# One tile per double chunk for the gated unit's input, and an order of its own for the first four double chunks

## The chip, the cores and the metric

The kernel runs on one core of a Trainium2 chip. A core has engines that run on their own and wait for one another by semaphores: TensorE (PE: matmuls and transposes, with its weight loads shown apart as PEld), VectorE (DVE), ScalarE (ACT), GpSimd (POOL) and SyncE (SP), which here only issues transfers. Matmuls write to PSUM[...]; everything else lies in SBUF. The metric is the device time of one execution in microseconds, a median of several. The span of a profiled execution, from its first to its last instruction, is a little shorter than its time.

## The reference

Eight batches, eight heads, 576 tokens, head size 64. Attention without softmax: scores are weighted by a decay per head and cut causally. Its output is laid out as x with 512 features, and a gated unit follows. The gate is a causal convolution over five tokens, so it needs the four tokens ahead of each stretch.

```python
scores = scale * (q @ k.transpose(0, 1, 3, 2))             # q, k, v: (8, 8, 576, 64)
gamma = 1 - 2.0 ** (-5.0 - arange(8))                      # one decay per head
ret = scores * where(rel >= 0, gamma ** rel, 0)            # rel = query position - key position
x = (ret @ v).transpose(0, 2, 1, 3).reshape(8, 576, 512)

xp = concatenate([zeros((8, 4, 512)), x], axis=1)
gate = sigmoid(sum(conv_w[k] * xp[:, k:k + 576] for k in range(5)))
out = (gate * (x @ w_val)) @ w_out                         # float32
```

## The kernel before

Work is cut into 18 double chunks, numbered m. A batch has two full ones of 256 tokens, and the four batches of a group share one of tails (4 x 64 tokens), so m = 8 and m = 17 are tails and the others are full. For a full one, each half `ab` of 128 tokens has masked scores within the half, and a running state of all halves before it for the rest.

For each m:

- `load` and `cast_*`: q, k, v arrive as float32 and become bfloat16, mostly on POOL; v is multiplied by a decay (`gin`).
- `turn`, `take_turned`: TensorE transposes k and q into PSUM and ACT copies them out (`kq`).
- `scores`, `masks`: 16 small matmuls into two banks, and DVE multiplies by the mask.
- `update`, `take_state`: the state grows by k times v of a half; ACT copies it out (`sd`, `sl`).
- `carried`, `values`: state times q, and masked scores times v, into the banks `o`.
- `take_x`: DVE multiplies `o` by the decay of the query (`gout`) and writes x as bfloat16.

One iteration later `conv` (the convolution, as matmuls with diagonal matrices `dg`), `gate`, `value` (x times w_val, then times the gate) and `project` (times w_out) follow. So iteration m mixes the attention of m with the gated unit of m-1 and the projection of m-2. The program's order on each engine is the order written here.

In the code `dcs[m]` gives (kind, batch or group, c), and c is the position of a full chunk in its batch: 0 at even and 1 at odd m in the first group; in the second group, after the tail, 0 at odd and 1 at even m.

```python
P, HP, W, PAD, GB, R = 128, 64, 256, 4, 4, 2      # W: tokens of a double chunk; PAD: leading tokens; GB: batches of a group
NP, NCH, TAIL, LB = 4, 2, 64, 4                   # NP: pairs of heads; NCH: full double chunks of a batch; LB: buffers of a load
# PSUM pools: ps_t, ps_s, ps_o, ps_st have one bank for each tile name; ps_g has two banks
    xg = [xp.tile([P, GB, NP, PAD + S], BF16, name=f"xg{g}") for g in range(B // GB)]
# ... (cut)
    def prep_wv(copy, part):
        src = wvf.rearrange("p o (pr ab hl j) -> p o pr ab hl j", pr=2, ab=2, hl=2)
        for (j0, blk, ab, hl) in ORDER[2 * part:2 * part + 2]:
            copy(wvb[:, :, blk:blk + 2, j0:j0 + HP], src[:, :, :, ab, hl, :])
# ... (cut)
    def take_x(m, ab):
        kind, b, c = dcs[m]
        if kind == "full":
            t0 = c * W + ab * P
            nc.vector.tensor_tensor(
                xg[b // GB][:, b % GB, :, PAD + t0:PAD + t0 + P].rearrange("p o (n r) -> p o r n", r=R),
                ops[m, ab], gout[:, :, t0:t0 + P].rearrange("p o (r n) -> p o r n", r=R), op=ALU.mult)
        else:
            nc.vector.tensor_tensor(
                xg[b][:, ab::2, :, PAD + c * W:PAD + S].rearrange("p b o n -> p o b n"),
                ops[m, ab], gout[:, :, c * W:S].unsqueeze(2).to_broadcast([P, NP, R, TAIL]), op=ALU.mult)
# ... (cut)
    def take_state(m, ab):

        if m >= ND or dcs[m][0] != "full":
            return
        kind, b, c = dcs[m]
        last = ab == 1 and c == NCH - 1
        t = tp_sb.tile([P, NP, D], BF16, name="sl" if last else "sd", bufs=GB if last else 4)
        nc.scalar.copy(t, st[b])
        before[("tail", b) if last else (m, 1) if ab == 0 else (m + 1, 0)] = t

    def xs(n, rows, blk, shift):
        kind, b, c = dcs[n]
        c0 = c * W + shift
        if kind == "full":
            return xg[b // GB][rows, b % GB, blk, c0:c0 + W]
        return xg[b][rows, :, blk, c0:c0 + TAIL]

    gps, gsb, zsb = {}, {}, {}

    def conv(n):

        g = [ps_g.tile([P, 2, 2 * P], F32, name="g") for _ in range(2)][::-1]
        gps[n] = g
        gsb[n] = {}
        lists = [], []
        for pr in range(2):
            a, b = 2 * pr, 2 * pr + 1
            for kk in range(KC):
                for bank, rows, blks in ((0, half[1], (b, a)), (1, half[0], (a, b))):
                    lists[bank].append([mm(g[bank][half[i], pr, :], lhsT=dg[rows, blks[i], kk, :],
                                           rhs=xs(n, rows, blks[i], kk), start=(pr == 0 and kk == 0),
                                           stop=(pr == 1 and kk == KC - 1)) for i in range(2)])
        return lists

    def gate(n, i):
        t = gp.tile([P, 2, 2 * P], F32, name=f"gate{i}")
        nc.scalar.activation(t, gps[n][i], AF.Sigmoid)
        gsb[n][i] = t

    def value(n, i, bank=None):
        vps = (spare(ps_g, "g") if bank is None else bank).rearrange("p (j n) -> p j n", j=2)
        for j in range(2):
            for o in range(NP):
                nc.tensor.matmul(vps[:, j, :], lhsT=wvb[:, o, 2 * i + j, :], rhs=xs(n, slice(0, P), o, PAD),
                                 start=(j == 0 and o == 0), stop=(j == 1 and o == NP - 1), skip_group_check=True)
        z = gp.tile([P, 2, 2 * P], BF16, name=f"z{i}", bufs=3)
        nc.vector.tensor_tensor(z, gsb[n][i], vps, op=ALU.mult)
        zsb[n, i] = z
# ... (cut)
    def keep_warm(n):

        t = ps_t.tile([P, DM], F32, name="tps")
        for _ in range(n):
            nc.tensor.matmul(t, zeros[:, 0:P], zeros, start=True, stop=True)

    keep_warm(8)
    cast_k(0, (v_copy, 4))
    bank = turn(0, 0)
    take_turned(0, 0, bank, (v_copy, 4))
    cast_q(0, (s_copy, 2), (g_copy, 2))
    prep_conv_weights()
    keep_warm(4)
    bank = turn(1, 0, spare(ps_g, "g", [P, NP, R, P], BF16))
    take_turned(1, 0, bank, (s_copy, 2), (v_copy, 2))
    prep_gout(0)
    cast_v(0)
    for o in range(2):
        prep_diagonals(o, nc.vector)
    for (name, f) in (("k", cast_k), ("q", cast_q), ("v", cast_v)):
        f(1)
    for m in range(LB, LB + 2):
        for name in "kqv":
            load(name, m)

    pairs = lambda a: [sum(a[k:k + 2], []) for k in range(0, len(a), 2)]
    for m in range(ND + 1):
        now, unit, nxt, last = ok(m), ok(m - 1), ok(m + 1), m == ND
        soon = m < 2

        if now:
            run(scores(m, 0))
            masks(m, 0, 0)
            masks(m, 0, 1)
        if m == 0:
            keep_warm(4)
            run(update(0, 0))
            take_state(0, 0)
            for o in range(2, NP):
                prep_diagonals(o, nc.vector)
        hi, lo = conv(m - 1) if unit else ([], [])
        if now:
            run(carried(m, 1))
            run(pairs(update(m, 1)), lo[0:2])
            take_state(m, 1)
        else:
            run(lo[0:2])
        run(lo[2:10], hi[0:8])
        if unit:
            gate(m - 1, 1)
        if soon:
            run(hi[8:10])
        else:
            run(pairs(update(m + 1, 0)), hi[8:10])
            take_state(m + 1, 0)
        if unit:
            gate(m - 1, 0)
        if now:
            run(scores(m, 1))
            masks(m, 1, 0)
            masks(m, 1, 1)

        if last:
            value(m - 1, 1, spare(ps_s, "s1"))
            value(m - 1, 0, spare(ps_s, "s0"))
            project(m - 2, 0)
            project(m - 2, 1)
            project(m - 1, 0, last=True)
            project(m - 1, 1, last=True)
            continue
        if m == 1:
            prep_wv(v_copy, 1)
            prep_wv(s_copy, 0)
            value(0, 1)
        if nxt:
            bank = turn(0, m + 1)
            take_turned(0, m + 1, bank)
        if m > 1:
            value(m - 1, 1)
            project(m - 2, 0)
        if ok(m + 2):
            for (name, f) in (("k", cast_k), ("q", cast_q), ("v", cast_v)):
                f(m + 2)
                if ok(m + 2 + LB):
                    load(name, m + 2 + LB)

        run(*values(m, 1))
        run(*values(m, 0))
        run(carried(m, 0))
        take_x(m, 0)
        take_x(m, 1)

        if nxt:
            bank = turn(1, m + 1)
            take_turned(1, m + 1, bank)
        if m == 0:
            prep_gout(1)
            nc.scalar.activation(warm, lsc, AF.Sigmoid)
            load_wo()
        if unit:
            value(m - 1, 0)
        if ok(m - 2):
            project(m - 2, 1)
        if soon:
            run(update(m + 1, 0))
            take_state(m + 1, 0)
```

## Time and profile before

| | before |
|---|---|
| time, median of 3 | 181.7 us (179.49 to 183.25) |
| span of the profiled execution (its time: 180.84) | 179.1 us |
| mean granted TensorE clock | 0.958 of full speed |
| bytes moved, mean rate | 39.81 MB, 222 GB/s |
| of it read, written | 30.42 MB, 9.44 MB |

The costliest groups on the engines, as the page's fifth part gives them (busy time of all, and one instruction's mean):

| operation | engine | count | busy us | one, ns |
|---|---|---|---|---|
| mask times scores (L294) | DVE | 64 | 41.2 | 685 |
| value matmuls (L408, in bank g) | PE | 272 | 37.4 | 277 |
| transposed k, q out of PSUM (L272) | ACT | 34 | 34.6 | 1019 |
| projection (L418) | PE | 111 | 34.7 | 379 |
| v times decay, to bfloat16 (L242) | POOL | 18 | 34.5 | 1916 |
| convolution matmuls (L254, dg) | PE | 720 | 31.4 | 280 |
| decay times o, written as x (L343) | DVE | 32 | 22.3 | 745 |

How to read such a profile: a busy time is the sum of an engine's instructions, and says nothing of when they ran. The rows of 40 slices show when, in tenths of each slice. A row of a timeline has a start, a length, the engine, the line of the program, the operation, what it writes and reads, and how many instructions were merged; in square brackets stands how long the engine was idle before it and whose work it then waited for. TensorE's small matmuls overlap one another, so their single durations don't add up.

### The profile page before, as it was taken

The numbers are of one execution on the slowest core, as the hardware profiler recorded it, in microseconds if no ns is written. First come the engines' busy times: TensorE is split into PE (matmuls) and PEld (weight loads), VectorE is DVE, ScalarE is ACT, GpSimd is POOL, SyncE is SP. The second block draws the span as 40 slices with busy tenths as digits, with TensorE's granted clock in tenths as the row PEclk, the third lists the DMA queues.
The fourth block names the chain that finished last, engine by engine and source line by source line (L and its number), as shares of the span: only waits on it lengthen the run. The fifth ranks groups of instructions, "written<-read, shape, count | busy, mean of one in ns | idle before, by whom it ended". The sixth has DMA issues, their size and how long they took to land.

```text
span 179.1 us, 7593 instructions
## 1 busy us (share of the span) xinstructions
PE 148.3 (83%) x3344; PEld 108.8 (61%) x3377; DVE 105.9 (59%) x191; ACT 93.4 (52%) x154; POOL 74.0 (41%) x69
## 2 busy tenths in 40 slices
PE   7776370889889998998978997999899899989980
PEld 2344270776657685766756775777577576757630
DVE  6468409356566675666445775766667576665320
ACT  3163843256465674665356563756476565633330
POOL 4372499487645446281708263562805000000000
PEclk9999558699999999999999999999999999999998
DMA  4999999999897799999999697876842111111334
GB/s 140 347 321 249 343 287 248 314 299 298 252 254 176 224 330 346 286 344 305 332 345 300 222 289 203 261 227 152 200 168 109 61 65 59 62 62 65 114 117 117
DMA packets 69054, 39.81 MB, mean 222 GB/s; under 512 B 14218, under 2 KB 63902, under 8 KB 69022
## 3 DMA queue, kind: packets, MB, share of 16 engines
q1 hardware_dynamic: 68256, 38.54, 73.2%
q0 software_dynamic: 576, 0.52, 1.8%
q8 instruction: 26, 0.43, 1.0%
q10 hardware_dynamic: 190, 0.27, 0.6%
q14 instruction: 6, 0.05, 0.1%
HBM read 30.42 MB, written 9.44 MB: 222 GB/s over the span
## 4 chain that ended last, share of the span: by engine, by line
PE 74%; DVE 13%; ACT 4%; issue 4%; DMA 2%; ACTq 0%; DVEq 0%
PE g L408 18%; PE g L418 16%; PE g L254 13%; PE tps L264 9%; PE o L308 8%; DVE xg L343 6%; PE s L254 6%; PE st L254 3%; DMA fk<-in_k_dram 2%; DVE wvb L217 2%; DVE p L294 2%; DVE dg L211 2%; ACT gout L187 1%; PE s L408 1%; PE tps L442 1%
## 5 line engine op out<-in xcount | busy, mean ns | idle before, releaser
L294 DVE TENSOR_TENSOR p<-s,mask 128x512 bf16<-128x512 f32 x64 | 41.2, 685 | 22.3 <-PE s L254 22.3
L272 ACT COPY kq<-tps 128x1024 bf16<-128x1024 bf16 x34 | 34.6, 1019 | 23.0 <-PE tps L264 22.8
L408 PE MATMUL g<-xg,wvb 128*128 128x256 bf16 x272 | 37.4, 277 | 10.2 <-DVE xg L343 5.4
L226 POOL CAST qb<-fq 128x1024 bf16<-128x1024 f32 (+1 forms) x18 | 18.3, 1019 | 49.9 <-issue 21.7
L418 PE MATMUL g<-wob,z 128*128 128x512 bf16 x111 | 34.7, 379 | 2.1 <-issue 0.4
L426 ACT COPY ob<-g 128x512 f32<-128x512 f32 x34 | 19.9, 585 | 31.3 <-PE g L418 27.9
L242 POOL TENSOR_TENSOR vb<-fv,gin 128x1024 bf16<-128x1024 f32 x18 | 34.5, 1916 | 3.6 <-DMA fv<-in_v_dram 3.5
L408 PEld LDWEIGHTS <-wvb 128*128 128x128 bf16 x288 | 26.8, 99 | 14.9 <-issue 7.2
L411 DVE TENSOR_TENSOR z<-gate,g 128x512 bf16<-128x512 f32 x34 | 23.4, 687 | 17.6 <-PE g L408 17.6
L254 PE MATMUL g<-xg,dg 64*64 64x256 bf16 x720 | 31.4, 280 | 0.8 <-issue 0.6
L343 DVE TENSOR_TENSOR xg<-o,gout 128x512 bf16<-128x512 f32 x32 | 22.3, 745 | 12.0 <-PE o L308 12.0
L401 ACT ACTIVATE gate<-g 128x512 f32<-128x512 f32 x36 | 21.2, 604 | 13.6 <-DVE p L294 7.1
L254 PEld LDWEIGHTS <-dg 64*64 64x64 bf16 x720 | 24.1, 109 | 3.6 <-issue 3.1
L226 POOL CAST kb<-fk 128x1024 bf16<-128x1024 f32 x17 | 17.8, 1050 | 8.8 <-DMA fk<-in_k_dram 6.7
L418 PEld LDWEIGHTS <-z 128*128 128x128 bf16 x144 | 14.0, 98 | 10.4 <-issue 0.6
L254 PE MATMUL s<-kq 64*64 64x128 bf16 (+1 forms) x576 | 17.6, 222 | 2.4 <-ACT kq L272 1.2
L254 PEld LDWEIGHTS <-kq 64*64 64x64 bf16 x576 | 12.6, 109 | 9.6 <-issue 9.6
L254 PE MATMUL st<-vb,kb 64*64 64x64 bf16 x512 | 13.9, 196 | 0.0
L308 PEld LDWEIGHTS <-vb 64*64 64x64 bf16 x576 | 8.6, 107 | 8.8 <-issue 8.7
L308 PE MATMUL o<-kq,sd 64*64 64x128 bf16 x192 | 9.4, 222 | 4.7 <-ACT sd L371 4.0
L254 PEld LDWEIGHTS <-kb 64*64 64x64 bf16 x512 | 12.4, 112 | 0.8 <-issue 0.8
L308 PE MATMUL o<-p,vb 64*64 64x128 bf16 (+1 forms) x576 | 11.4, 216 | 1.6 <-DVE p L294 1.6
(65 smaller groups left out, 108.2 us busy)
## 6 DMA issues: line engine op xcount, KB each, us to landing
fk<-in_k_dram SPq DMA_DIRECT2D x16, 512.0 KB, 6.1
fq<-in_q_dram SPq DMA_DIRECT2D x16, 512.0 KB, 7.1
fv<-in_v_dram SPq DMA_DIRECT2D x16, 512.0 KB, 7.2
out_dram<-ob SPq DMA_DIRECT2D x32, 256.0 KB, 3.6
wvf<-in_moe_w_val_dram SPq DMA_DIRECT2D x4, 256.0 KB, 6.2
fk<-in_k_dram SPq DMA_DIRECT2D x8, 128.0 KB, 3.4
fq<-in_q_dram SPq DMA_DIRECT2D x8, 128.0 KB, 3.8
fv<-in_v_dram SPq DMA_DIRECT2D x8, 128.0 KB, 3.4
```

The lines of the kernel that those rows point to most:

```text
L226: copy(t[:, o:o + n], src[:, o:o + n])
L242: eng.tensor_tensor(vbf[m][:, h:h + n], loaded["v", m][:, h:h + n], g[:, h:h + n].unsqueeze(3).to_broadcast([P, n, R, D]), op=ALU.mult)
L254: return lambda: nc.tensor.matmul(*a, skip_group_check=True, **kw)
L272: copy(kq[m][:, which, o:o + n], bank[:, o:o + n])
L294: nc.vector.tensor_tensor(p[:, :, 0:n], sps[m, r][i][:, :, 0:n], mask[dcs[m][0], r].unsqueeze(1).to_broadcast([P, NP, n]), op=ALU.mult)
L308: nc.tensor.matmul(o, start=key not in opened, stop=False, skip_group_check=True, **kw)
L343: nc.vector.tensor_tensor(xg[b // GB][:, b % GB, :, PAD + t0:PAD + t0 + P].rearrange("p o (n r) -> p o r n", r=R), ops[m, ab], gout[:, :, ...
L401: nc.scalar.activation(t, gps[n][i], AF.Sigmoid)
L408: nc.tensor.matmul(vps[:, j, :], lhsT=wvb[:, o, 2 * i + j, :], rhs=xs(n, slice(0, P), o, PAD), start=(j == 0 and o == 0), stop=(j == 1 and ...
L411: nc.vector.tensor_tensor(z, gsb[n][i], vps, op=ALU.mult)
L418: nc.tensor.matmul(o, lhsT=zsb[n, j // 2][:, j % 2, i * P:(i + 1) * P], rhs=wob[:, j, :], start=(j == 0), stop=(j == NP - 1))
L426: nc.scalar.copy(ob, o)
```

## The change

x was kept in one tile per group, `xg[g]`, with all positions of four batches. Now there is one tile per group and chunk position, `xg[g][c]`, with its own four leading tokens. For c = 0 they are zeros; for the others the new `pass_on` has POOL copy the last four tokens of the tile before. A write of one chunk's x and a read of another chunk's are thereby in different tiles.

The first double chunk leaves the loop and gets an order of its own, to follow the inputs as they arrive, and m = 1 to 3 keep the loop but with another order in its first half (`late`). In particular:

- the table of query decays `gout` is made at once, ahead of the first input, in four activations of 576 instead of eight of 256 and 320, and the sigmoid's table is loaded right after q(0) is copied out;
- `cast_q(0)` is one POOL instruction, not halves on ACT and POOL;
- the warming matmuls (`keep_warm`) write a bank of the `o` pool, not the transposes' bank, and there are fewer at a time;
- both `scores(0, r)` come together, the second in the two `g` banks;
- the two transposes of m = 1 stand ahead of `values(0)`;
- half of w_val is cast on POOL (`prep_wv(g_copy, 1)`) where DVE did it in iteration 1; w_out's loads are issued between the casts of m = 2;
- in m = 1 to 3 the convolution of m-1 comes first and both state updates of m after most of it, where the first update had been at the end of the iteration before or beside the convolution; from m = 4 on the order is the old one;
- at the very end both halves of the convolution run interleaved, and both gates follow.

The transfers of q, k, v, w_val, w_out and the output are the same, and so is the arithmetic.

```diff
@@ -178,12 +178,9 @@
                                 lrow.unsqueeze(1).unsqueeze(3).to_broadcast([P, NCH + 1, H, R]), op=ALU.mult)
-        nc.scalar.activation(gin, gin, AF.Exp)
         gout = consts.tile([P, NP, S], F32, name="gout")
+        for pr in range(NP):
+            nc.scalar.activation(gout[:, pr, :], posi, AF.Exp, bias=lsc, scale=lcol[:, pr:pr + 1])
+            if pr == 1:
+                nc.scalar.activation(gin, gin, AF.Exp)
         warm = consts.tile([P, 1], F32, name="warm")
-        def prep_gout(part):
-            cs = slice(part * W, S if part else W)
-            for pr in range(NP):
-                nc.scalar.activation(gout[:, pr, cs], posi[:, cs], AF.Exp, bias=lsc, scale=lcol[:, pr:pr + 1])
         identf = consts.tile([32, 32], F32, name="identf")
@@ -192,5 +189,7 @@
         nc.vector.tensor_copy(id2, idb)
-        xg = [xp.tile([P, GB, NP, PAD + S], BF16, name=f"xg{g}") for g in range(B // GB)]
+        xg = [[xp.tile([P, GB, NP, PAD + (W if c < NCH else TAIL)], BF16, name=f"x{g}{c}") for c in range(NCH + 1)]
+              for g in range(B // GB)]
         for t in xg:
-            nc.vector.memset(t[:, :, :, 0:PAD], 0.0)
+            nc.vector.memset(t[0][:, :, :, 0:PAD], 0.0)
         new_bank = lambda: ps_t.tile([P, NP, R, P], BF16, name="tps")
@@ -281,4 +280,5 @@
-        def scores(m, r):
-            s = [ps_s.tile([P, NP, P], F32, name=f"s{i}") for i in range(2)]
+        def scores(m, r, spare=False):
+            s = [ps_g.tile([P, NP, P], F32, name="g") if spare else ps_s.tile([P, NP, P], F32, name=f"s{i}")
+                 for i in range(2)]
             sps[m, r] = s
@@ -341,5 +341,5 @@
             if kind == "full":
-                t0 = c * W + ab * P
+                t0, x0 = c * W + ab * P, PAD + ab * P
                 nc.vector.tensor_tensor(
-                    xg[b // GB][:, b % GB, :, PAD + t0:PAD + t0 + P].rearrange("p o (n r) -> p o r n", r=R),
+                    xg[b // GB][c][:, b % GB, :, x0:x0 + P].rearrange("p o (n r) -> p o r n", r=R),
                     ops[m, ab], gout[:, :, t0:t0 + P].rearrange("p o (r n) -> p o r n", r=R), op=ALU.mult)
@@ -347,4 +347,11 @@
                 nc.vector.tensor_tensor(
-                    xg[b][:, ab::2, :, PAD + c * W:PAD + S].rearrange("p b o n -> p o b n"),
+                    xg[b][c][:, ab::2, :, PAD:].rearrange("p b o n -> p o b n"),
                     ops[m, ab], gout[:, :, c * W:S].unsqueeze(2).to_broadcast([P, NP, R, TAIL]), op=ALU.mult)
+        def pass_on(m):
+            kind, b, c = dcs[m]
+            if kind == "full":
+                x = xg[b // GB]
+                nc.gpsimd.tensor_copy(x[c + 1][:, b % GB, :, 0:PAD], x[c][:, b % GB, :, W:W + PAD])
@@ -376,6 +383,5 @@
             kind, b, c = dcs[n]
-            c0 = c * W + shift
             if kind == "full":
-                return xg[b // GB][rows, b % GB, blk, c0:c0 + W]
-            return xg[b][rows, :, blk, c0:c0 + TAIL]
+                return xg[b // GB][c][rows, b % GB, blk, shift:shift + W]
+            return xg[b][c][rows, :, blk, shift:shift + TAIL]
@@ -439,3 +445,3 @@
-            t = ps_t.tile([P, DM], F32, name="tps")
+            t = ps_o.tile([P, NP, R, HP], F32, name="o0").rearrange("p o r n -> p (o r n)")
             for _ in range(n):
@@ -448,11 +454,10 @@
         take_turned(0, 0, bank, (v_copy, 4))
-        cast_q(0, (s_copy, 2), (g_copy, 2))
+        cast_q(0)
         prep_conv_weights()
-        keep_warm(4)
+        prep_diagonals(0, nc.vector)
+        keep_warm(3)
         bank = turn(1, 0, spare(ps_g, "g", [P, NP, R, P], BF16))
         take_turned(1, 0, bank, (s_copy, 2), (v_copy, 2))
-        prep_gout(0)
+        nc.scalar.activation(warm, lsc, AF.Sigmoid)
         cast_v(0)
-        for o in range(2):
-            prep_diagonals(o, nc.vector)
         for (name, f) in (("k", cast_k), ("q", cast_q), ("v", cast_v)):
@@ -462,2 +467,36 @@
                 load(name, m)
+        prep_wv(g_copy, 1)
+        keep_warm(3)
+        run(scores(0, 0))
+        masks(0, 0, 0)
+        masks(0, 0, 1)
+        run(scores(0, 1, spare=True))
+        masks(0, 1, 0)
+        masks(0, 1, 1)
+        keep_warm(2)
+        run(update(0, 0))
+        take_state(0, 0)
+        keep_warm(1)
+        run(update(0, 1))
+        take_state(0, 1)
+        run(carried(0, 1))
+        prep_diagonals(1, nc.vector)
+        prep_diagonals(2, nc.vector)
+        bank = turn(0, 1)
+        take_turned(0, 1, bank)
+        bank = turn(1, 1)
+        take_turned(1, 1, bank)
+        run(*values(0, 1))
+        run(*values(0, 0))
+        run(carried(0, 0))
+        take_x(0, 0)
+        take_x(0, 1)
+        pass_on(0)
+        for (name, f) in (("k", cast_k), ("q", cast_q)):
+            f(2)
+            load(name, LB + 2)
+        load_wo()
+        cast_v(2)
+        load("v", LB + 2)
+        prep_diagonals(3, nc.vector)
@@ -466,5 +505,6 @@
         pairs = lambda a: [sum(a[k:k + 2], []) for k in range(0, len(a), 2)]
-        for m in range(ND + 1):
-            now, unit, nxt, last = ok(m), ok(m - 1), ok(m + 1), m == ND
-            soon = m < 2
+        for m in range(1, ND + 1):
+            now, nxt, last = ok(m), ok(m + 1), m == ND
+            late = m < 4
+            hi, lo = conv(m - 1)
@@ -474,10 +514,16 @@
                 masks(m, 0, 1)
-            if m == 0:
-                keep_warm(4)
-                run(update(0, 0))
-                take_state(0, 0)
-                for o in range(2, NP):
-                    prep_diagonals(o, nc.vector)
-            hi, lo = conv(m - 1) if unit else ([], [])
-            if now:
+            if last:
+                run(lo, hi)
+                gate(m - 1, 1)
+                gate(m - 1, 0)
+            elif late:
+                run(lo[0:8], hi[0:8])
+                run(pairs(update(m, 0)), hi[8:10])
+                take_state(m, 0)
+                gate(m - 1, 0)
+                run(pairs(update(m, 1)), lo[8:10])
+                take_state(m, 1)
+                gate(m - 1, 1)
+                run(carried(m, 1))
+            else:
                 run(carried(m, 1))
@@ -485,13 +531,6 @@
                 take_state(m, 1)
-            else:
-                run(lo[0:2])
-            run(lo[2:10], hi[0:8])
-            if unit:
+                run(lo[2:10], hi[0:8])
                 gate(m - 1, 1)
-            if soon:
-                run(hi[8:10])
-            else:
                 run(pairs(update(m + 1, 0)), hi[8:10])
                 take_state(m + 1, 0)
-            if unit:
                 gate(m - 1, 0)
@@ -511,3 +550,2 @@
             if m == 1:
-                prep_wv(v_copy, 1)
                 prep_wv(s_copy, 0)
@@ -531,2 +569,3 @@
             take_x(m, 1)
+            pass_on(m)
@@ -535,11 +574,6 @@
                 take_turned(1, m + 1, bank)
-            if m == 0:
-                prep_gout(1)
-                nc.scalar.activation(warm, lsc, AF.Sigmoid)
-                load_wo()
-            if unit:
-                value(m - 1, 0)
-            if ok(m - 2):
+            value(m - 1, 0)
+            if m > 1:
                 project(m - 2, 1)
-            if soon:
+            if m == 3:
                 run(update(m + 1, 0))
```

## The prediction

> **What bounds the kernel now.** The page first: its busy shares, the rows of 40 slices (4.5 us each) and the shares of the chain that ended last.
>
> ```profile
> PE 148.3 (83%) x3344; PEld 108.8 (61%) x3377; DVE 105.9 (59%) x191; ACT 93.4 (52%) x154; POOL 74.0 (41%) x69
> ...
> PE   7776370889889998998978997999899899989980
> ...
> PEclk9999558699999999999999999999999999999998
> ...
> PE 74%; DVE 13%; ACT 4%; issue 4%; DMA 2%; ACTq 0%; DVEq 0%
> ```
>
> TensorE carries the chain. It is full from slice 8 on; before that stand a 3, a 7 and a 0, and the granted clock falls to half. So there are two stretches: a ragged start and a dense rest. The table of stretches, cut where an iteration's first scores start, measures both (columns: stretch, length, busy time of PE, PE's weight loads, DVE, ACT, POOL, with counts; granted clock; DMA share; GB/s).
>
> ```profile
> 19.60:28.20 8.60, 4.05 (x96) 3.56 (x95) 2.57 (x5) 6.26 (x12) 6.59 (x8) 0.54 1.07 306
> 28.20:37.30 9.10, 5.06 (x74) 3.85 (x76) 5.29 (x6) 2.11 (x3) 6.79 (x5) 0.81 1.12 283
> 37.30:45.66 8.36, 7.66 (x203) 5.84 (x208) 5.93 (x9) 4.61 (x8) 6.27 (x6) 1.00 1.06 297
> 45.66:54.91 9.25, 7.74 (x194) 5.67 (x200) 5.33 (x8) 4.82 (x8) 5.52 (x4) 1.00 0.90 240
> 54.91:62.35 7.44, 7.33 (x186) 5.60 (x192) 5.36 (x8) 4.93 (x8) 2.87 (x4) 1.00 0.78 204
> 62.35:70.75 8.40, 7.50 (x194) 5.70 (x200) 5.33 (x8) 4.82 (x8) 5.04 (x4) 1.00 1.09 334
> ```
>
> Iteration 1 takes the first two rows, 17.7 us. Iteration 4 (an even chunk, 54.91) takes 7.44 with PE busy for 7.33; iteration 5 (odd) takes 8.40 with 7.50 busy. That alternation repeats to the end. The timeline says what fills the holes.
>
> ```profile
> 19.44 2.29 ACT L187 ACTIVATE gout<-posi,lsc,lcol 128x320 f32<-128x320 int32 x4
> ...
> 21.73 1.28 ACT L538 ACT_TABLE_LOAD   x1
> ...
> 23.13 0.35 ACT L371 CAST sd<-st 128x256 bf16<-128x256 f32 x1
> 23.54 0.19 PEld L308 LDWEIGHTS <-sd 64*64 64x64 bf16 x8 [3.54 <-ACT sd L371]
> ...
> 28.12 3.31 DVE L217 CAST wvb<-wvf 128x512 bf16<-128x512 f32 x2
> ...
> 31.49 1.89 PE L408 MATMUL g<-xg,wvb 128*128 128x256 bf16 x8 [4.53 <-DVE wvb L217]
> ```
>
> Two holes in iteration 1: a state copy queued on ACT behind decay tables and a table load (3.3 to 3.5 us of PE), and the first value matmuls behind the DVE cast of half of w_val (4.53). In the dense part:
>
> ```profile
> 51.69 1.38 DVE L343 TENSOR_TENSOR xg<-o,gout 128x512 bf16<-128x512 f32 x2 [0.79 <-PE o L308]
> ...
> 52.04 0.27 PE L408 MATMUL g<-xg,wvb 128*128 128x256 bf16 x1
> ...
> 53.12 0.93 PE L408 MATMUL g<-xg,wvb 128*128 128x256 bf16 x7 [0.81 <-DVE xg L343]
> ```
>
> The value matmuls read the chunk before and need nothing of this x. Yet the first of eight runs and seven wait 0.81 us for DVE's second write. The four 128-token blocks of a chunk's x lie 580 apart in xg, so the span from the first to the last byte of the write overlaps what matmuls 2 to 8 read, and not what the first reads: the wait comes of sharing the tile. It occurs at odd chunks only (same batch, same tile); at even ones the batches differ.
>
> [...] 128x512 matmuls take 0.43 us each at the start, 0.26 in the group at 11.45, and the clock is 0.50 from 18 to 26 us. [...]
>
> **The change part by part.** Start of each step estimated from durations above; m is the number of the double chunk.
>
> First the dense part. A tile for each chunk position removes the 0.81 us at odd chunks m = 5, 7, 10, 12, 14, 16 (1 and 3 count with the start). Is PE then free? An odd iteration becomes 8.40 - 0.81 = 7.59, still above its 7.50 of PE work; DVE has 5.33 and ACT 4.82, so nothing else fills it. Sum: 6 x 0.81 = 4.9 us. Added: 16 copies of four tokens on POOL. The smallest POOL copy in the trace, posi from ti, 128x64, took 0.24, so at most 0.24 each, 3.8 in all, on an engine busy for 74 of 179 us. Such a copy waits for x(m), and POOL's casts for m+3 queue behind it. They take 1.04 + 1.04 + 1.90 = 4.0 us, and PE wants the first of them more than an iteration later. No cost.
>
> Now the start. Before x(0): q(0) is cast by POOL alone, 6.32 + 1.04 = 7.36 instead of 6.93; but the warming matmuls no longer write the transposes' bank, so they do not wait for DVE's copy (0.56), and there are three, not four: the q transposes start at about 8.1 instead of 9.0. Scores end near 10.6, both row sets together in separate banks. Their four masks (four times 0.635) run to about 13.2; state copies follow on ACT. Both transposes of m = 1 now stand ahead of the value products and share one bank, so the second waits for ACT's 1.01 us copy: near 13.5 to 14.6, PE idles. The products follow at 15.2 to 16.5, and x(0) is done at about 17.9 (before: 17.40 + 1.37 = 18.8). Gain there: under 1 us.
>
> Decay tables move ahead of everything: four activations of 576. From 0.52 (256 wide) and 0.57 (320 wide) the slope is 0.86 ns an element, so 0.79 each, 3.2 in all, plus 0.24 for gin; from the table's end at 2.75 they finish near 6.2, when ACT has nothing else. The sigmoid table follows near 10. The w_val half goes to POOL after v(1), 12.77 + 1.90 = 14.7, its transfer landed by about 17 at the latest (issued 7.80 to 11.2, 6.2 to landing): ready before 19, needed after 22.
>
> Iteration 1: scores near 17; conv(0) waits for x(0), 17.9, and I assume half clock, so 2 us, to 20.2. Two state updates in a row, each behind an ACT copy (0.37 and the gate 0.6 between), carried products and second scores: to 22.1. The value product wants a bank that a gate has to read, 22.5, and runs to 24.4 at half clock; turn and value products to 25.8; x(1) to 27.2; second turn and value(0,0) to 27.6. So iteration 2 starts at about 27.6, against 37.3 before: 9.7 earlier. That is 10.6 us for an iteration that took 17.7.
>
> Do inputs allow it? In the trace POOL casts k(2) at 18.5, q(2) at 21.2, v(2) at 22.65, each on a transfer's landing. After, the issue of w_out's four loads (2.54 us on POOL) comes ahead of v(2): cast to about 26.7, needed at about 29. Then k, q, v(3) to 30.7, needed from 31; v(4) lands at 35.7 as before, needed near 43; v(6) at 45.9, needed near 58. Transfers are close but not last.
>
> Iterations 2 and 3 in the new order: 7.44 plus about 0.75 for the second state update that waits for ACT's read of the first, 8.2 each: iteration 4 at 27.6 + 16.4 = 44.0, against 54.9. Start gain: 10.8 us. The end (both convolution banks interleaved, gates behind) moves a few tenths either way: 0.
>
> Sum: 10.8 + 4.9 = 15.7. Span 179.1 - 15.7 = 163.4; time 181.7 - 15.7 = **166.0 us**.
>
> **The rivals.** One: the start is set by transfers. For it: DMA's share is 1.07 to 1.15 from 6 to 45 us. Against: the last two landings that hold POOL up, v(5) at 40.2 and v(6) at 45.9, are wanted only near 50 and 58 in my schedule. If they did bind, iteration 4 would start near 48 and the time be 170. Two: the half clock persists. The state-update waits and the shared transpose bank leave gaps of 0.5 to 1 us in iterations 1 to 3; if the clock stays at 0.5 there, PE's 7.4 us become 10 or more and half the start gain goes: 171. Were it never to fall, I'd gain 3 more: 163. Three: the token copies make POOL a link of PE's chain: POOL may no longer run ahead, and a wait for POOL takes the 0.81's place. For it: in-order POOL stands at each copy until x is there. Against: more than one iteration of slack; the page has POOL finishing at slice 30 of 40. Then only the start would count: 171. Four: the odd waits are real data waits after all. Against: the first of eight matmuls doesn't wait, and even chunks don't.
>
> **Range and chances.** The 4.9 is well measured; of the start, 7.8 us are two named holes that move off PE's path, and the rest is my schedule, good to 4 us. Three runs before spread from 179.5 to 183.3. So 161.5 to 170.5. No rival takes more than about 6 of 15.7, and 2% is 3.6: faster 0.95, same 0.03, slower 0.02.
>
> **What would show it.** Value matmuls at odd chunks that follow the transposes without a wait for x, and stretches of 7.4 and 7.6 us alternating; no wait for DVE's wvb; iteration 2's first scores near 27.6 and iteration 4's near 44; clock dips at most once after 16 us. I am wrong if PE waits for POOL's x or casts, if iterations 2 and 3 exceed 9 us, or if PE waits on inputs of m = 2 or 3.

## The result, and the profile after

The changed kernel takes 171.3 us (median of 4 runs) against 180.6 for the kernel before; the ratio is 0.947, 95% interval 0.933 to 0.962 (ratios are of the runs within 1.5% of their kernel's fastest). A second series gave 170.6 against 180.4, ratio 0.937 (0.931 to 0.942). So the change brings some 9 to 10 us of the 15.7 that were predicted, and the time lies just above the range.

The trace that came with the first series (span 171.0) is of the slowest of its four runs; all lines of the changed kernel below are of one from the second series, span 166.9, whose time of 168.6 us is 2 under the median of that series. The page, with the same rows as before:

```profile
PE 148.6 (89%) x3378; PEld 107.9 (65%) x3378; DVE 102.6 (61%) x189; ACT 91.7 (55%) x149; POOL 77.4 (46%) x87
...
PE   6895898798999959899988999899999999999970
...
PEclk9999569999999999999999999999999999999996
DMA  4999999999997799999999999998872111131134
...
PE 66%; DMA 13%; issue 7%; SPq 3%; POOL 3%; ACT 3%; DVE 2%; ACTq 0%; POOLq 0%; DVEq 0%
```

The 3, 7 and 0 of the start are gone. But the chain has lost its DVE share (13 to 2%) and gained DMA 13%, issue 7% and SPq 3%: it runs through transfers and through moments in which PE waits for nothing the profile shows. The DMA row is at 7 or more up to slice 30 of 40 (125 us), and PE's row is all 9s only from slice 27 (108 us) to slice 38.

The table of stretches, cut at first scores as before, iterations 1 to 5:

```profile
16.60:26.70 10.10, 8.70 (x168) 7.29 (x168) 5.35 (x10) 4.79 (x8) 7.83 (x11) 0.66 1.06 305
26.70:36.05 9.35, 8.02 (x187) 5.68 (x186) 5.80 (x9) 4.36 (x7) 6.43 (x7) 1.00 1.11 284
36.05:44.70 8.65, 8.01 (x209) 5.92 (x212) 5.34 (x8) 5.07 (x9) 6.58 (x7) 1.00 1.08 319
44.70:52.60 7.90, 7.54 (x202) 5.70 (x197) 5.33 (x8) 4.97 (x9) 3.95 (x5) 1.00 1.01 283
52.60:61.90 9.30, 7.50 (x193) 5.67 (x192) 5.33 (x8) 4.72 (x8) 5.44 (x7) 1.00 0.84 214
```

Iteration 1 takes 10.1 us where it took 17.7, at a clock of 0.66, and iteration 4 starts at 44.7 where it started at 54.9. Then iteration 5, an odd one that should take 7.6, takes 9.3. The timeline shows that the wait it had is gone (rows at 58 us):

```profile
57.82 1.38 DVE L343 TENSOR_TENSOR x<-o,gout 128x512 bf16<-128x512 f32 x2 [0.79 <-PE o L308]
...
58.18 1.04 PE L414 MATMUL g<-x,wvb 128*128 128x256 bf16 x8
```

All eight value matmuls run together, while DVE still writes the other chunk's x. What came in its place, in the same trace:

```profile
57.40 1.04 SPq L434 DMA_DIRECT2D out_dram<-ob  x2
...
60.37 0.59 ACT L432 COPY ob<-g 128x512 f32<-128x512 f32 x1 [3.79 <-DMA out_dram<-ob]
61.01 1.02 PE L424 MATMUL g<-wob,z 128*128 128x512 bf16 x4 [1.80 <-ACT ob L432]
...
105.03 0.24 PE L253 MATMUL s<-kq 64*64 64x128 bf16 x2 [0.69 <-issue]
```

First, ACT stands idle for 3.79 us, in the end for want of an output buffer: the landing of an output at 60.3 ends the wait. The outputs were not issued before 57.4: SP was busy from 47.6 to 57.3 with the twelve issues of the tail's loads, which stand ahead of them in its order. PE then waits 1.80 for ACT. Second, stalls called issue in the middle of a run of 16 equal matmuls, 0.69 here.

Two stretches of iterations, the same in both kernels, show where the gain went: m = 4 to 11, while the queues are full of loads, and m = 12 to 16, when the loads run out (the last one, for the tail m = 17, lands at 124.6 us in the changed kernel and at 130.8 in the kernel before). The changed kernel, then the kernel before:

```profile
45.20:110.90 65.70, 60.50 (x1504) 45.30 (x1506) 41.63 (x64) 38.15 (x63) 31.89 (x32) 1.00 1.02 304
110.90:148.00 37.10, 37.10 (x946) 28.30 (x939) 26.71 (x40) 23.84 (x40) 15.29 (x16) 1.00 0.44 134
```

```profile
55.30:120.20 64.90, 59.74 (x1485) 45.03 (x1490) 41.66 (x64) 38.21 (x63) 30.36 (x24) 1.00 0.94 283
120.20:160.20 40.00, 37.06 (x936) 28.18 (x939) 26.67 (x40) 23.83 (x40) 8.76 (x7) 1.00 0.36 108
```

In the second stretch the new tiles bring 40.0 - 37.1 = 2.9 us, with PE busy for every one of the 37.1. In the first they bring nothing: 65.7 against 64.9, at 304 instead of 283 GB/s. Together with the start, (55.3 - 45.2) + (64.9 - 65.7) + 2.9 = 12.2 us, and that is the difference of the two spans, 179.1 - 166.9.

The stalls called issue are not new. The kernel before has them in the same stretch, of 0.35, 0.89, 0.57 and 0.71 us, 2.5 in all; the changed kernel has 2.9 there. Two rows of the kernel before:

```profile
92.87 0.28 PE L308 MATMUL o<-kq,sl 64*64 64x64 bf16 x9 [0.89 <-issue]
...
109.52 0.24 PE L308 MATMUL o<-kq,sd 64*64 64x128 bf16 x2 [0.71 <-issue]
```

What is new in this pair of traces is the 1.80 us wait for an output buffer. It takes the place of the waits for x, which were 0.80, 0.82 and 0.18 us in this stretch: the issue stall of 0.71 us stands just before the third.

### The profile page after: what moved, and what is told of

Its sections match the earlier page's. It is cut to its first block, busy times and chain, and to the rows that moved or that the text cites. A ratio compares the mean times of both kernels' runs of the same rounds, so it can differ in the third digit from the quotient of the medians.

```text
span 171.0 us, 7633 instructions
## 1 busy us (share of the span) xinstructions
PE 150.2 (88%) x3378; PEld 108.7 (64%) x3378; DVE 102.7 (60%) x189; ACT 91.6 (54%) x149; POOL 77.3 (45%) x87
## 3 DMA queue, kind: packets, MB, share of 16 engines
HBM read 30.42 MB, written 9.44 MB: 233 GB/s over the span
## 4 chain that ended last, share of the span: by engine, by line
PE 63%; DMA 13%; SPq 6%; issue 6%; DVE 5%; POOL 3%; ACT 2%; ACTq 0%; POOLq 0%; DVEq 0%
PE g L424 15%; PE g L414 14%; PE g L253 11%; PE tps L263 8%; PE o L308 6%; DMA fq<-in_q_dram 6%; SPq L92 5%; PE s L253 5%; DMA fv<-in_v_dram 4%; DMA fk<-in_k_dram 2%; POOL vb L241 2%; PE st L253 2%; DMA out_dram<-ob 2%; PE o L448 2%; DVE dg L210 1%
## 5 line engine op out<-in xcount | busy, mean ns | idle before, releaser
L294 DVE TENSOR_TENSOR p<-s,mask 128x512 bf16<-128x512 f32 x62 | 40.0, 686 | 24.0 <-PE s L253 24.0
L271 ACT COPY kq<-tps 128x1024 bf16<-128x1024 bf16 x34 | 34.6, 1018 | 18.0 <-PE tps L263 17.7
L424 PE MATMUL g<-wob,z 128*128 128x512 bf16 x144 | 37.4, 386 | 1.9 <-ACT ob L432 1.9
L414 PE MATMUL g<-x,wvb 128*128 128x256 bf16 x272 | 36.2, 277 | 0.2 <-ACT gate L407 0.2
L253 PE MATMUL g<-x,dg 64*64 64x256 bf16 x720 | 31.8, 280 | 1.2 <-DVE x L343 0.5
L343 DVE TENSOR_TENSOR x<-o,gout 128x512 bf16<-128x512 f32 x32 | 22.1, 743 | 14.5 <-PE o L308 14.5
L356 POOL COPY x<-x 128x16 bf16<-128x16 bf16 x16 | 3.2, 197 | 59.8 <-DVE x L343 51.8
L225 POOL CAST qb<-fq 128x1024 bf16<-128x1024 f32 x18 | 18.8, 1042 | 5.5 <-DMA fq<-in_q_dram 5.5
L253 PE MATMUL s<-kq 64*64 64x128 bf16 (+1 forms) x560 | 16.4, 220 | 3.7 <-issue 3.0
L225 POOL CAST kb<-fk 128x1024 bf16<-128x1024 f32 x17 | 17.7, 1042 | 2.7 <-DMA fk<-in_k_dram 2.4
L253 PEld LDWEIGHTS <-kq 64*64 64x64 bf16 x576 | 11.8, 108 | 11.2 <-issue 10.4
L308 PE MATMUL o<-p,vb 64*64 64x128 bf16 (+1 forms) x576 | 12.0, 222 | 1.9 <-issue 1.9
```

What stands on the lines that cost most here:

```text
L225: copy(t[:, o:o + n], src[:, o:o + n])
L253: return lambda: nc.tensor.matmul(*a, skip_group_check=True, **kw)
L271: copy(kq[m][:, which, o:o + n], bank[:, o:o + n])
L294: nc.vector.tensor_tensor(p[:, :, 0:n], sps[m, r][i][:, :, 0:n], mask[dcs[m][0], r].unsqueeze(1).to_broadcast([P, NP, n]), op=ALU.mult)
L308: nc.tensor.matmul(o, start=key not in opened, stop=False, skip_group_check=True, **kw)
L343: nc.vector.tensor_tensor(xg[b // GB][c][:, b % GB, :, x0:x0 + P].rearrange("p o (n r) -> p o r n", r=R), ops[m, ab], gout[:, :, t0:t0 + P ...
```

## The experiments

Three theories of the missing part: **transfers** (PE loses time through output buffers and late fetches of its own instructions, because the queues are full), **POOL** (the token copies hold it back), **order** (iterations 1 to 3 cost more than thought). Times are medians. The kernels were measured in three groups, each beside runs of the kernel before: 180.4 us for the first four, 180.3 for the second four (loads that nobody reads, the order alone, outputs from ACT's queue, bursts), 179.5 for the rest.

**The changed kernel again.**

> The changed kernel once more, unaltered, for a second look at its trace. Three theories of where 6.4 us of the predicted 15.7 went. Transfers: from 30 to 115 us the DMA queues are full, and PE pays for it twice, by late fetches of its own instructions (stalls that the trace calls issue: 1.04, 0.90, 0.85 and 2.75 us) and by output transfers that stand behind loads on the SP queue until ACT has no output buffer (PE 1.95 us at 61). POOL: the token copies hold POOL back (51.8 us of waits for x), so casts and loads come later. Order: the new order of iterations 1 to 3 costs more than 8.2 us each. Transfers expects issue stalls of some 4 to 8 us in all before 115 us and none over 0.3 us after it, not all at the same places as in the first trace; time 169.5 to 172.5. The other two expect the first trace's stalls at the same places.

170.6 us. Issue stalls of 0.74, 0.84, 0.61 and 0.69 between 66 and 105 us, none over 0.3 after: 2.9 us in all, where 4 to 8 were expected. Three of the four stand at the same instructions as stalls of the first trace, with other lengths (0.74 for 0.90, 0.84 for 0.85, 0.69 for 2.75), so their places don't speak for transfers alone. The packets of the queue that the view of DMA calls instruction do. The trace holds 26 of them, of 16384 bytes each, for PE's 6773 instructions, some 260 apiece. Set beside the stalls (first trace, this one, and three kernels told below; the last column counts the instructions that PE had begun by then, weight loads included):

```text
stall of PE called issue     last instruction packet ended     stall's end after that     begun by then
first    32.49 to  33.53          32.09                            1.44                    961
first    67.23 to  68.13          66.77                            1.36                    2497
first   104.78 to 107.53         106.11                            1.42                    4289
again    83.09 to  83.93          82.32                            1.61                    3265
again   104.34 to 105.03         103.71                            1.32                    4289
ob8      84.62 to  87.09          85.65                            1.44                    3521
traffic  85.55 to  87.09          85.75                            1.34                    3521
lb3      79.46 to  80.81          79.26                            1.55                    3265
```

All 39 issue stalls of 0.5 us or more found after 15 us in the traces of this study end 1.2 to 1.6 us after such a packet was through, though packets are some 5 us apart. And their places are those of blocks: the counts in the last column differ by multiples of 256 (each is 193 more than one), and so do those of all 35 stalls in the traces that lack no records. The other four are the kernel before's, whose trace lacks some 30 of 6773. I infer, as the records don't show the fetch itself, that PE stopped where a block of 256 instructions ended and went on when the next had come: it ran out of instructions.

The packets themselves are no slower when the queues are full: 0.93 us is the median of those numbered 6 to 16 here, and 1.22 in the run without loads told below. They come later. When such a packet starts, PE is 141 instructions short of the block's end here, and 218 without loads (medians).

**Eight output buffers.**

```diff
-    op_sb = ctx.enter_context(tc.tile_pool(name="osb", bufs=5))
+    op_sb = ctx.enter_context(tc.tile_pool(name="osb", bufs=8))
```

> Eight output buffers in place of five, nothing else. Transfers: ACT no longer waits for an output buffer and PE's 1.95 us at 61 us goes, at most 0.3 us of it comes back as another wait; the time falls by 1.5 to 2 us (ratio to the changed kernel 0.99). POOL and order: no change, within 0.5 us.

167.4 us, 3.3 under the changed kernel measured beside it; against the kernel before 0.922 (0.914 to 0.930). The rows of the second projection of iteration 5 in its trace:

```profile
58.78 1.03 PE L424 MATMUL g<-wob,z 128*128 128x512 bf16 x4
...
59.84 0.58 ACT L432 COPY ob<-g 128x512 f32<-128x512 f32 x1 [0.72 <-PE g L424]
...
87.09 0.35 PE L253 MATMUL s<-kq 64*64 64x128 bf16 x9 [2.47 <-issue]
```

Here PE no longer waits for ACT, nor ACT for a transfer, and iteration 5 takes 7.44 by first masks where it took 9.40. The gain is larger than the 1.80 removed; the times of both kernels scatter by 5 us, so the excess isn't explained. The issue stalls stay (2.47 at 87).

**Loads of m = 6 and later left out.** The output is another, as those casts read the tiles of m = 4 and 5; the engines' work stays.

```diff
         def load(name, m):
+            if m >= 6:
+                loaded[name, m] = loaded[name, 4 + m % 2]
+                return
```

> The loads of m = 6 and later are left out; their casts read the tiles of m = 4 and 5, so the output is another, and every engine's work but the transfers is the same. Transfers: with the queues all but empty from about 45 us, all iterations from m = 4 take 7.4 to 7.6 us (the tails some 8), no issue stall over 0.3 us and no wait for output buffers after 50 us; iteration 4 starts at about 45 as before and the span is 45 + 4 x 7.5 + 8 + 8 x 7.5 + 18.9 = 162, time 164. POOL: the token copies stay, so the iterations stay as long as in the changed kernel, and the time within 2 us of 171. Order: the same 171.

162.0 us. The two stretches and, of the view of waits, POOL's row for the token copies:

```profile
44.50:104.20 59.70, 59.42 (x1508) 45.12 (x1512) 41.57 (x65) 38.06 (x63) 31.85 (x32) 1.00 0.21 74
104.20:141.30 37.10, 37.10 (x944) 28.29 (x937) 26.69 (x41) 23.83 (x40) 15.14 (x16) 1.00 0.20 74
```

```profile
POOL x L359 <- DVE x L346: 34.8, 8, 7.3
```

At 74 GB/s instead of 304, m = 4 to 11 take 59.7 us, 6.0 less, and PE is busy for 59.4 of them. The token copies still wait for x for 34.8 us, and in these stretches it costs nothing: the POOL theory falls. Iterations 1 to 3 take 28.5 us together where they took 28.0, so the new order costs what it cost, and the missing part lies behind them: the order theory can explain 1 us or so, not 9. The four times lie within 0.8 us; those of the changed kernel scatter over 5.9. So the traffic makes much of the scatter too. (Without the loads SP has less to issue as well, so outputs leave sooner: the one of 60.0 us is issued 0.03 after its copy ends, where the one of 61.9 in the changed kernel is issued 0.96 after; the next experiment puts that back.)

**Loads made, but read by nobody.** As the last, with the loads of m = 6 and later going to two spare sets of tiles; six output buffers, for space.

```diff
-            t = ld.tile([P, H, R, D], F32, name=f"f{name}")
+            t = (sink if m >= 6 else ld).tile([P, H, R, D], F32, name=f"{'u' if m >= 6 else 'f'}{name}")
             fetch(nc.sync, t, {"q": q, "k": k, "v": v}[name], m)
-            loaded[name, m] = t
+            loaded[name, m] = loaded[name, 4 + m % 2] if m >= 6 else t
```

> As noload, the casts of m = 6 and later read the tiles of m = 4 and 5, but the loads are made, into two spare sets of tiles that nothing reads; six output buffers. So no engine ever waits for these loads; only the traffic of the DMA queues is back. If PE loses time because its instruction fetches share the queues: issue stalls of 0.5 to 3 us come back between 45 and 115 us, 3 to 7 us in all with the slow clock after them, and the time is 164.5 to 169, against 162.0 without the traffic. If the loss was waiting for input data behind the casts: 162 to 163, as without the loads. Output buffers may cost up to 1 us.

167.6 us, some 5.6 more than without the traffic, though no engine waits for the data of these loads. Its two stretches:

```profile
44.70:108.70 64.00, 60.30 (x1504) 45.35 (x1506) 41.53 (x64) 38.17 (x64) 31.88 (x32) 1.00 1.01 299
108.70:145.80 37.10, 37.10 (x946) 28.28 (x939) 26.69 (x40) 23.80 (x40) 15.19 (x16) 1.00 0.54 164
```

64.0 against 59.7 us for the same matmuls, with stalls of 1.37 (a convolution's bank in PSUM that ACT hasn't emptied, for want of an output buffer) and 1.54 (issue) and smaller ones. The 3 to 7 us of issue stalls that were expected did not come. The loss is traffic, not late inputs, and instructions are only a part of it.

**The kernel before, loads of m = 6 and later left out.** The same edit.

> The kernel before with the loads of m = 6 and later left out, as in noload; the output is another, the engines' work the same. If the predicted sum was right but for the traffic, the change without traffic brings 15.7 us: 162.0 + 15.7 = 177.7, so 176.5 to 179 here; that is only 2 to 4 us under the 180.4 with the traffic, where the changed kernel gained 9. All x waits of 0.8 stay, iterations from m = 4 alternate 7.44 and 8.4, no issue stall after 50. If the traffic costs both kernels alike: 171 to 173.

178.4 us: without the traffic the change brings 178.4 - 162.0 = 16.4 us, close to the predicted 15.7. The kernel before loses only 1 to 2 us to the traffic, the changed one 9. Its stretches:

```profile
55.60:117.90 62.30, 59.88 (x1512) 44.91 (x1502) 41.64 (x65) 38.25 (x63) 30.39 (x25) 1.00 0.20 70
117.90:157.90 40.00, 37.59 (x944) 28.19 (x936) 26.66 (x41) 23.84 (x40) 8.69 (x7) 1.00 0.19 69
```

62.3 against 64.9 with all loads, and the second stretch unchanged. The trace has no issue stall over 0.3 us; the 2.5 us of them that the kernel before has in this stretch are of the size of its loss of 2.6.

**Each half of the change alone.** The new tiles with their token copies in the old order (its diff is the change's hunks for `xg`, `take_x`, `pass_on` and `xs`), and the new order with one tile per group and no copies.

> The kernel before with the new tiles and the token copies on POOL, in its old order at the start. By the prediction's sum it gains 8 x 0.81 = 6.5 us (two of the eight waits lie in iterations 1 and 3), so 174. Transfers: less than that, 3 to 5 us, as iterations that would be shorter while the queues are full stall elsewhere; after 115 us each odd chunk gains its full 0.8 to 1.0. POOL: 2 us or less, and also after 115 us no gain.

> The changed kernel with x in one tile per group again and no token copies: the new start alone. By the prediction's sum the start brings 10.8 us: 180.4 - 10.8 = 169.6. If the traffic takes a part of what is gained early: more, 171 to 175, with the 0.8 us waits for x back at odd m from 5 on and output-buffer and issue stalls between them.

175.6 and 175.3 us. In the traces the tiles alone take 37.1 us for m = 12 to 16, as in the full change, but 69.4 for m = 4 to 11 (53.6 to 123.1), with issue stalls of 1.84, 1.35, 0.57 and 1.66; that was the slowest of its six runs (171.3 to 180.8). The order alone starts iteration 4 at 45.4 and then takes 69.1 for m = 4 to 11, where the kernel before takes 64.9, and 40.0 for m = 12 to 16. So each half gives back a part while the loads run: by the medians they bring 4.8 and 5.0 of 6.5 and 10.8, the first of them uncertain by its scatter.

**Outputs from ACT's queue**, with eight buffers.

```diff
-                nc.sync.dma_start(out=out[u, c * W + i * P:c * W + (i + 1) * P, :], in_=ob)
+                nc.scalar.dma_start(out=out[u, c * W + i * P:c * W + (i + 1) * P, :], in_=ob)
```

> Eight output buffers, and the full chunks' outputs issued from ACT's queue, so that they no longer stand behind loads on SP's. Were the queue order on SP still costing anything beyond the buffers, 1 us or more faster than eight buffers alone (166.3 in its fast runs). If only instruction fetches are left: within 1 us of it, with ACT 0.5 us busier for each of 32 issues but not on PE's path.

180.0 us: a miss, by 13. The timeline at 38 us:

```profile
37.69 0.38 ACTq L434 DMA_DIRECT2D out_dram<-ob  x1
...
38.12 1.01 ACT L271 COPY kq<-tps 128x1024 bf16<-128x1024 bf16 x1 [5.46 <-DMA fk<-in_k_dram]
...
39.18 0.52 PE L253 MATMUL s<-kq 64*64 64x128 bf16 x16 [4.18 <-ACT kq L271]
```

ACT was idle for 5.46 us ahead of a copy that needs no transfer. Just before it in the timeline stands ACT's own output issue, from 37.69 to 38.07. The issue was not slow: all 32 on ACT took 0.34 to 0.39 us. It came late, and the row says what it waited for, the landing of a load of k. The trace's records show why: in this program the loads of q, k, v and w_val and the outputs take eight semaphores in turn, and an issue first waits until the transfer that had its semaphore before has landed (in the first trace of the changed kernel they are eight of the numbers 100 to 110, and ahead of the issue at 22.91 stands a wait for number 102, set before by the load of w_val that was issued at 9.94 and landed at 16.6). Here that was a load issued at 31.55, which landed at 37.61. At 44.3 the next output waits likewise for a load of q issued at 37.64. On ACT such a wait held up PE for 4.18 us, and again for 3.21 at 45: the iterations m = 2 to 4 take 38.8 us by first masks, 12.9 more than with eight buffers alone, which is the size of the whole loss. So the run doesn't tell what SP's queue order costs beyond the buffers.

**Bursts and lookahead.** With eight output buffers: v's load moved behind the iteration's second output, and three or two load buffers in place of four (`LB = 3`, `LB = 2`).

> Eight output buffers, and each load of v (m = 6 and later) issued after the iteration's second output, no longer right behind k and q: at most 1 MB of loads in a row in place of 1.5. If fetches are late because they queue behind such bursts: fewer or shorter issue stalls between 50 and 115 us than with eight buffers alone (0.52, 2.47, 1.65 there), and 1 to 3 us faster, 163.5 to 165.5. If bursts don't matter, only the mean rate: within 1 us of 166.3.

> Eight output buffers and three buffers for loads in place of four, so that loads run five ahead of their use and not six; the bytes spread over one more iteration. If the density of the traffic makes the issue stalls: 0.5 to 1.5 us faster than eight output buffers alone (167.4 median, 166.3 in fast runs). If lookahead matters for inputs: slower, with POOL waiting for loads.

> The same with two buffers for loads: four ahead. From 45 us on some 20.5 MB over about 80 us, 256 GB/s, where four buffers give 21 MB over 65 us, 323 GB/s, of the 345 seen at most. Density of the traffic: fewer issue stalls, 164 to 166 median, the last loads near 125 us. Lookahead: POOL's casts wait for loads in the first iterations, iteration 4 starts 1 us or more later than 45, and the time is 168 or more.

168.6, 165.9 and 168.5 us, where eight buffers alone took 167.4. Issue stalls remain in all three, the longest of 1.92, 1.35 and 1.26 us. Within the scatter of 5 to 6 us that each of them has, bursts don't matter, and three or two buffers are not told apart from four. The fastest version run, 165.9, is eight output and three load buffers: below both kernels, but only the output buffers' part is clear. In its trace m = 4 to 11 take 62.8 us with all loads made, at 304 GB/s, so that rate by itself doesn't forbid the gain.

## Why the prediction was wrong

**The step that failed** is "First the dense part": "Is PE then free? An odd iteration becomes 8.40 - 0.81 = 7.59 ... so nothing else fills it", with its term 6 x 0.81 = 4.9 us. I asked only the engines, not the queues. The wait itself went as told, and from m = 12 on the term is even too small: 2.9 us for the three odd chunks 12, 14 and 16, 0.97 each. While the queues were full it came out as -0.8 us instead of 3 x 0.81 = 2.4; without the traffic it would have been 62.3 - 59.7 = 2.6. The kernel moved 283 GB/s in that stretch already, and a shorter iteration needs more in the same time: 304, where the fullest slice of the first trace's page has 347. Two things that I had not in the sum fill the time: waits for output buffers, new with the change (1.80 us), and issue stalls, late instructions as I read them, which were there before it (2.5 us) and didn't shrink with it (2.9 us in the trace shown, 4.5 in the first). They are part of the "issue 4%" of the page, which the prediction shows and passes over. Together they are 4.7 of the 6.0 us by which the stretch exceeds that without loads; the rest are smaller losses that the traces don't tell apart.

In the two traces the sum came out at 12.2 us, short by 0.7 at the start and by 2.8 in the dense part. By the medians, 9.3 and 9.8, the change brings less, as other runs of the changed kernel lose more to the traffic: the first trace takes 69.5 us for m = 4 to 11.

**The start**: predicted 10.8 us, measured 10.1 to 10.2 on first scores and masks. Iteration 2 starts at 26.7 (predicted 27.6), iteration 4 at 44.7 (44.0). The clock did fall, as assumed, to a mean of 0.66 in iteration 1, and came back to 1.00 from 26.7 on. Iteration 2 cost more than its 8.2, 9.35, and more than the 9 that was to be a sign of being wrong: PE waited 0.87 us for w_out and 0.42 for ACT's read of the state; iteration 3, 8.65. These two terms are mis-sized by 18.0 - 16.4 = 1.6 us, and what lay ahead of them was 0.9 better than told.

**Rival one** ("the start is set by transfers") named the right resource and, in the main, the wrong place. The objection to it, that inputs land early enough, was true of q, k and v but not of w_out, for which PE waited 0.87 us. And inputs are not all that DMA moves: 9.44 MB of outputs and 0.43 MB of instruction packets went with them.

**Rival two**, the clock: in runs whose clock never fell before 30 us (with loads left out, with loads that nobody reads, and with three load buffers) iteration 4 started at 44.5, 44.7 and 44.9, hardly earlier than 45.2, all by the first masks; what PE gained it spent waiting for POOL's half of w_val (1.46, 1.34 and 1.35 us) and for w_out (1.45, 1.85 and 1.82). So the 3 us for a warm clock were wrong too. **Rival three**, POOL: refuted by the run without loads. **Rival four**, real data waits: refuted by the timeline. Two small readings of the prediction were off, without effect: the fifth value matmul reads the same block as the first and only stands in order behind the second, and POOL's last busy slice is 31, not 30.

So the missing mechanism, late blocks of instructions, is my reading of two measurements: the packets of 16384 bytes that end ahead of each stall, and places that differ by multiples of 256 instructions. It cost nothing at 74 GB/s, where no issue stall over 0.3 us appears after 45 us; at the 294 of the first trace (m = 4 to 11) it cost up to 2.75 us at one block.

**What stays open**: what makes the packets start later while loads run, as they take no longer themselves, and so what would avoid the stalls. In all traces that lack no records a packet starts with at most 290 instructions left, about one block ahead. Moving one load in three and running fewer loads ahead did not show it. That each half of the change loses several us to the traffic, and that eight output buffers bring more than the wait that they remove, is measured and not explained beyond the higher rate.

## What to carry to other kernels

Before adding up waits to be removed, ask of each stretch what DMA still has to move in the shorter time: here the new tiles gained nothing at 283 GB/s and all of their waits once the loads ran out. The outputs, and the 26 instruction packets too, were moved by DMA like the inputs, and PE was stopped for up to 2.75 us with no data to wait for. Stalls with nothing to wait for, at places a multiple of 256 PE instructions apart, as all 35 were that could be counted, point to late blocks of instructions. Leaving loads out while the engines' work stays shows in one run how much of a time the traffic costs: 9 us here, of which three more output buffers took back 3. And before an engine is made to issue transfers, look at what its issues would wait for: one held ACT up for 5.46 us.

## What the runs showed of the hardware, unexpected

- All 39 issue stalls of PE ended 1.2 to 1.6 us after a 16384-byte instruction packet, and the 35 that could be counted stood at the same place of a block of 256 instructions. In the changed kernel's two traces none over 0.3 us came after 107.6 us, and there was none in the two runs with loads left out.
- A long stall cost more than its length: after the four of 1.84 us and more (1.84, 1.92, 2.47, 2.75) the granted clock was 0.50 for 3.4 us. Of the five from 1.54 to 1.73 us, one was followed by that.
- While loads ran, SP took up to 2.23 us to issue one output in the first trace of the changed kernel, and 0.33 us for that at 60.0 with loads left out. With the outputs on ACT each issue took 0.34 to 0.39 us there, but one held ACT up for 5.46 us, as it waited for a load that had used its semaphore before.
- Two builds of diagonals on DVE took 2.25 us together at 13.0 us, while POOL multiplied v, and a single one 0.48 at 7.6 and at 16.7, all in the changed kernel. In the kernel before, DVE's two casts of w_val took 3.31 us together at 28.1, while POOL cast and multiplied too, and ACT's two of the same shape 1.14 at 27.2.
